# Convolution and low-rank mixer on one core: batch 0 cut in three pieces, index tables made between the loads, h of group 0 from four partial sums

## The chip, the core and the metric

The kernel runs on one core of a Trainium2 chip. The metric is device time in microseconds; the time before is the median of 11 runs, 331.04 us (330.2 to 332.82). One further execution was taken by the profiler and gave the trace; times "at 12.19" are microseconds from the start of its span. The core has TensorE (products, into eight PSUM banks of 128 x 512 fp32), VectorE, ScalarE and GpSimd (element work; GpSimd cannot be used on PSUM here and issues the loads that change type), and SyncE, which issues the other transfers. In the profile they are PE (PEld is its weight load), DVE, ACT, POOL and SP.

## The reference

`x` is 8 batches of 4224 rows of 192 numbers, in 8 heads of 24. A softmax over seven weights per head gives a causal convolution along the rows; its result `y` goes through a mixer of rank 32 over the rows and then a two-layer block per row:

```python
w = softmax(weight, axis=-1)                       # 8 heads x 7 taps
y[b, s] = sum over k of w[head, k] * x[b, s + k - 6]
h = y.transpose(0, 2, 1) @ U @ V                   # U 4224 x 32, V 32 x 4224
u = y + h.transpose(0, 2, 1)
out = u + maximum(u @ w_ch1, 0) @ w_ch2            # 192 -> 768 -> 192
```

The sum over rows in `y.T @ U` needs all of a batch's `y` before any `h` of that batch exists.

## The kernel before, in words

A batch is 33 tiles of 128 rows; eight tiles make a group, and 33 groups cover the eight batches. Group 0 and 1 hold tiles 0 to 15 of batch 0.

**Layout of x.** `x_sb` holds blocks of 64 rows: partitions 0 to 63 (r = 0) hold the first 32 blocks, partitions 64 to 127 (r = 1) the rest, plus one block of halo (L76 to L82). For batch 0 the loads are issued by GpSimd in pieces, `KP` (L86): tiles 0 to 12 of each half first, then the rest (tiles 13 to 15 of r = 0, 13 to 16 of r = 1).

**Queues.** The order of every engine is that of the program: nothing is rescheduled. GpSimd issues the two loads of the first piece (L95), makes the index tables with iota (L101 to L123), then issues U (L130, L134), the second piece of x (L135), V for groups 0 and 1 (L139), w_ch1 in four parts (L143), V for the rest (L153, L160), w_ch2 (L164) and batch 1 (L709). Its loads use eight completion semaphores in turn, so the ninth load waits until the first has landed, and so on. SyncE loads the weights (L61) and later only issues group transposes (L537) and outputs (L629).

**The convolution as products.** `hot` (L184) marks, from the tables `dif` and `tap`, where each tap stands in a 32 x 38 strip; `pr` is `hot` times the softmax weights, four heads at a time; seven products with the identity (L231) sum the taps in PSUM, and four ScalarE copies (L240) put the strips into `band`, a 128 x 128 matrix per head. `conv` (L368) multiplies `band` with blocks of x, 16 products of 64 x 64 per head for both halves of the partitions, and copies the result into `y_sb`: ScalarE for r = 0, VectorE for r = 1. Products of a zero tile (`idle`, L170) stand before the band and between band and convolution.

**U.** U is loaded with four rows in one partition; `u_layout` (L276) multiplies it with the selection matrix `Eq` (from the table `efp`) to get one row per partition, `U_sb`.

**Low-rank product.** `tt_mm` (L405) takes one product of 32 output rows per tile and puts them in turn in four column groups of the array, so that PSUM holds four partial sums in its four quarters of 32 partitions. For batches 1 to 7 `tt_split` (L421) writes them as a bf16 high part and low part, and `tt_sum` (L464) adds the quarters by products with `R4` (ones where two indices agree modulo 32) and copies the sum, repeated in all four quarters, to `tt_sb`. For batch 0 this is done otherwise: `tt_first` (L429) takes the first piece's 26 tiles, copies the partial sums to `tt_f` in fp32 and copies U of the last seven tiles four times side by side; after the rest of the convolution, an fp32 product with `R4f` (L701) and seven wide products (`tt_more`, L448) build the sum in PSUM, and `tt_done` copies it.

**Group 0 and 1.** `yT_part` (L542) puts the transposed `y` into three banks by products with the identity; `hT_part` (L558) adds h transposed there (V0_sb, 32 rows) and copies the sum to `uT`, one half by ScalarE, the other by VectorE. From group 2 on `h_group` makes u, and a DMA transposes it.

**The main loop** (L741): `w1` (L582) makes six pairs of 128 x 512 results per group, each reread with relu by ScalarE or VectorE; `w2` (L608) makes the output of two tiles, VectorE adds u, SyncE stores. An order written by hand (`SLOTS`) places the convolution and the low-rank steps of the next batches between these. After the first `w1` come `yT_part(1)`, `hT_part(1)` and h of group 2 (L753).

The start, which the edit rewrites, is this order:

Of the kernel before, what the change touches and what calls it, by code (L numbers as in the profile page):

```python
# [14 lines left out]
def kernel(  # L15
# [10 lines left out]
    nc = tc.nc  # L26
# [59 lines left out]
    KP = [(0, 13), (13, NB1 // 2)]  # L86

    def x_piece(k):
        for r in range(2):
            k0, k1 = KP[k]  # L90
            k1 = min(k1, (NB0, NB1)[r] // 2)
            x_part(0, r, (1 - r if k == 0 else 2 * k0 + 1), 2 * k1 + 1)

    x_tile(0)
    x_piece(0)  # L95
# [5 lines left out]
    dif = cst.tile([P, BW], F32, name="dif")  # L101
    for r in range(4):
        nc.gpsimd.iota(
            dif[QB * r : QB * r + QB, :],
            pattern=[[1, BW]],
            base=0,
            channel_multiplier=-1,
            allow_small_or_imprecise_dtypes=True,
        )
    tap = cst.tile([P, KC], F32, name="tap")  # L110
    nc.gpsimd.iota(
        tap[:],
        pattern=[[-1, KC]],
        base=HW,
        channel_multiplier=0,
        allow_small_or_imprecise_dtypes=True,
    )

    fp = cst.tile([P, P], I32, name="fp")
    nc.gpsimd.iota(fp[:], pattern=[[1, P]], base=P, channel_multiplier=-1)  # L120

    efp = cst.tile([P, 4, P], I32, name="efp")
    nc.gpsimd.iota(efp[:], pattern=[[-1, 4], [1, P]], base=4 * P, channel_multiplier=-4)  # L123
# [11 lines left out]
    x_piece(1)  # L135


    V0_sb = cst.tile([32, 2 * GT * P], BF16, name="V0_sb")
    nc.gpsimd.dma_start(out=V0_sb[:], in_=moe_V[:, 0 : 2 * GT * P])  # L139
    W1_sb = cst.tile([P, 3, M4], BF16, name="W1_sb")  # L140
    for m0, m1 in ((0, 2 * P), (2 * P, M4)):
        for hf in range(2):
            nc.gpsimd.dma_start(  # L143
                out=W1_sb[HB * hf : HB * hf + HB, :, m0:m1],
                in_=moe_w_ch1[:, m0:m1].rearrange("(c k) m -> k c m", k=HB),
            )

# [19 lines left out]
    zz = cst.tile([P, 512], BF16, name="zz")  # L167
    nc.vector.memzero(zz[:])  # L168

    def idle(n, w):  # L170
# [6 lines left out]
    idle(60, P)  # L177
# [5 lines left out]
    x_zero(0, nc.vector)  # L183
    hot = cst.tile([P, KC, BW], BF16, name="hot")  # L184
# [4 lines left out]
        op=ALU.is_equal,  # L189
    )  # L190
# [30 lines left out]
    def band_half(hh):  # L221
# [16 lines left out]
        for r in range(4):  # L238
            o = QB * (r % 2)
            nc.scalar.activation(  # L240
                out=band[QB * r : QB * r + QB, HQ * hh : HQ * hh + HQ, o : o + BW],
                in_=bp[QB * r : QB * r + QB, 0 : HQ * BW].rearrange("p (h t) -> p h t", h=HQ),
                func=ACT.Copy,
            )

    band_half(0)
    band_half(1)


    Eq = cst.tile([P, 4, P], BF16, name="Eq")  # L250
    nc.vector.tensor_scalar(
        out=efp[:], in0=efp[:], scalar1=P - 1, scalar2=None, op0=ALU.bitwise_and
    )
    nc.vector.tensor_scalar(
        out=Eq[:], in0=efp[:], scalar1=0.0, scalar2=None, op0=ALU.is_equal
    )
    nc.vector.tensor_scalar(
        out=fp[:], in0=fp[:], scalar1=R - 1, scalar2=None, op0=ALU.bitwise_and
    )
    R4f = cst.tile([P, P], F32, name="R4f")  # L260
    nc.vector.tensor_scalar(
        out=R4f[:], in0=fp[:], scalar1=0.0, scalar2=None, op0=ALU.is_equal
    )
    R4 = cst.tile([P, P], BF16, name="R4")
    nc.vector.tensor_copy(out=R4[:], in_=R4f[:])
# [10 lines left out]
    def u_layout():  # L276
        up = [bank() for _ in range(4)]
# [11 lines left out]
        for jj in range(4):  # L289
# [4 lines left out]
            )  # L294

# [72 lines left out]
    def conv(b, h0, nh, rs, engs, k0=0, k1=NT):  # L368
# [4 lines left out]
        pp = {r: bank() for r in rs}  # L373
# [31 lines left out]
    def tt_mm(b, js, p=None, o=0):  # L405
# [3 lines left out]
        for n, j in enumerate(js):  # L409
            c = n % 4  # L410
            nc.tensor.matmul(  # L411
                out=p[32 * c : 32 * c + 32, o : o + D],
                lhsT=U_sb[:, j // 4, j % 4, :],
                rhs=yt[b][:, j, :],
                start=(n < 4),
                stop=(n + 4 >= len(js)),
# [11 lines left out]

    def tt_first(p, js, rest):  # L429


        U4_sb = cst.tile([P, sum(b - a for a, b in rest), 4, R], BF16, name="U4_sb")
        n = 0
        for a, b in rest:
            nc.vector.tensor_copy(
                out=U4_sb[:, n : n + b - a, :, :],
                in_=U_sb[:]
                .rearrange("p k j r -> p (k j) r")[:, a:b, :]
                .unsqueeze(2)
                .to_broadcast([P, b - a, 4, R]),  # L440
            )
            n += b - a
        p = tt_mm(0, js, p, 256)
        t = sml.tile([P, D], F32, name="tt_f", bufs=1)
        evac("A", t[:], p[:, 256 : 256 + D])
        return U4_sb, t

    def tt_more(p, U4_sb, rest):  # L448
        js = [j for a, b in rest for j in range(a, b)]
        for n, j in enumerate(js):  # L450
            nc.tensor.matmul(
                out=p[:, 0:D],
                lhsT=U4_sb[:, n, :, :].rearrange("p a r -> p (a r)"),
                rhs=yt[0][:, j, :],
                start=False,
                stop=(n + 1 == len(js)),
            )
# [100 lines left out]
    def hT_part(g, tp, engs):  # L558

        uTt[g] = uts.tile([P, 4, 3, P], BF16, name="uT")  # L560
        for c in range(3):
            for hf in range(2):
                nc.tensor.matmul(
                    out=tp[c][HB * hf : HB * hf + HB, :],
# [234 lines left out]
```

## Time and profile before

| what | us |
|---|---|
| median of 11 runs | 331.04 (330.2 to 332.82) |
| the profiled execution | 329.99 |
| its span | 328.0 |
| first and second half of x land | 8.7 and 12.2 |
| band complete, first convolution product that has all of x's first piece | 11.14, 12.24 |
| first copy of uT of group 0 | 20.38 |
| first product of w1, group 0 | 21.27 |
| uT of group 1, first copy on the chain | 26.86 |
| first product of w2 | 32.30 |

The profile has a page (busy time per engine, the span in slices, DMA queues, the chain of work that ended last, the costliest groups of instructions) and views that answer questions: the chain in order of time (start, length, what), the instructions in order of time, groups by line and shape (count, busy time, mean ns of one), and for a line the durations of its instructions as least/median/greatest ns. A load's "to landing" counts from its issue.

### The profile page before, as it was taken

The page shows a single profiled execution, that of the slowest core. Times are in us where ns is not written, and L with a number is a line of the kernel's source. Part 1 is how long each engine was busy: PE and PEld are TensorE (multiplying, and loading weights), DVE is VectorE, ACT ScalarE, POOL GpSimd, SP SyncE. Part 2 cuts the span into 40 slices and gives each one's busy share as a digit, 9 for nine tenths or more (in the row PEclk, how much of TensorE's full clock was granted, in tenths as well). Part 3 has the DMA queues.
Part 4 walks back from the last instruction along what each step waited for, and adds up shares of the span by engine and source line. Part 5 has one row for each costly group of instructions (what it writes and reads, how often), then busy time and mean ns, then how long its engine had stood idle before and what let it go on. Part 6 is the DMA issues. An engine that isn't in the chain of part 4 may idle for free.

```text
span 328.0 us, 9736 instructions
## 1 busy us (share of the span) xinstructions
PE 318.6 (97%) x4072; PEld 224.5 (68%) x4072; DVE 268.5 (82%) x547; ACT 170.9 (52%) x351; POOL 142.1 (43%) x109
## 2 busy tenths in 40 slices
PE   7889999999999999999999999999999999999995
PEld 7655676567548746967874784587797497487494
DVE  5757999996986997898698799879897897896863
ACT  1658444662586098068529807833903902912910
POOL 8490229856993795967659598000000000000000
PEclk9999999999999999999999999999999999999999
DMA  8999996799999899699899969039569259259045
GB/s 99 192 164 166 165 208 153 144 193 164 244 176 231 144 204 190 175 218 182 170 222 155 203 172 199 27 98 250 65 128 218 91 144 215 78 129 258 3 131 160
DMA packets 122908, 53.54 MB, mean 163 GB/s; under 512 B 87760, under 2 KB 122832, under 8 KB 122864
## 3 DMA queue, kind: packets, MB, share of 16 engines
q1 hardware_dynamic: 84672, 38.18, 52.9%
q0 software_dynamic: 38192, 14.73, 39.5%
q8 instruction: 32, 0.52, 0.7%
q14 instruction: 12, 0.10, 0.1%
HBM read 29.49 MB, written 25.95 MB: 169 GB/s over the span
## 4 chain that ended last, share of the span: by engine, by line
PE 88%; DVE 4%; DMA 3%; ACT 3%; issue 1%; POOL 0%; DVEq 0%; POOLq 0%
PE ps L614 41%; PE ps L590 37%; PE ps L352 3%; DMA x_sb<-in_x_dram 3%; PE ps L496 3%; ACT rl_sb L601 2%; PE ps L411 2%; DVE y_sb L274 2%; DVE rl_sb L603 1%; DVE u_sb L518 1%; PE ps L381 0%; DVE out_sb L622 0%; POOL x_sb L79 0%; PE ps L467 0%; DVE uT L274 0%
## 5 line engine op out<-in xcount | busy, mean ns | idle before, releaser
L601 ACT ACTIVATE rl_sb<-ps 128x512 bf16<-128x512 f32 x235 | 125.3, 605 | 111.1 <-PE ps L590 99.1
L614 PE MATMUL ps<-W_sb,rl_sb 128*128 128x192 bf16 x1584 | 141.7, 246 | 0.1
L614 PEld LDWEIGHTS <-rl_sb 128*128 128x128 bf16 x1584 | 128.0, 98 | 13.4 <-issue 12.8
L590 PE MATMUL ps<-uT,W_sb 64*128 64x512 bf16 x1188 | 132.0, 376 | 0.8 <-DVE uT L274 0.8
L603 DVE TENSOR_SCALAR rl_sb<-ps 128x512 bf16<-128x512 f32 x161 | 104.3, 687 | 17.7 <-PE ps L590 17.4
L590 PEld LDWEIGHTS <-W_sb 64*128 64x128 bf16 x1188 | 64.2, 94 | 64.3 <-issue 5.0
L622 DVE TENSOR_TENSOR out_sb<-ps,u_sb 128x384 f32<-128x384 f32 (+1 forms) x133 | 70.1, 549 | 24.9 <-PE ps L614 24.5
L318 POOL COPY xb_sb<-x_sb 32x3072 bf16<-32x3072 bf16 (+1 forms) x24 | 67.6, 2824 | 0.7
L518 DVE TENSOR_TENSOR u_sb<-y_sb,ps 128x192 bf16<-128x192 bf16 (+1 forms) x168 | 66.2, 459 | 0.0
L306 POOL COPY xb_sb<-x_sb 128x3072 bf16<-128x3072 bf16 x12 | 32.8, 2742 | 30.6 <-DMA x_sb<-in_x_dram 12.9
L272 ACT ACTIVATE y_sb<-ps 128x384 bf16<-128x384 f32 (+3 forms) x90 | 36.8, 503 | 9.3 <-PE ps L352 6.8
L79 POOL DMA_DIRECT2D x_sb<-in_x_dram x32 | 27.1, 849 | 24.7 <-PE ps L590 14.4
L274 DVE CAST y_sb<-ps 128x408 bf16<-128x408 f32 (+2 forms) x42 | 20.8, 547 | 2.6 <-PE ps L381 2.6
L496 PE MATMUL ps<-tt_sb,V_sb 32*128 32x192 bf16 x264 | 12.6, 246 | 0.8 <-DVE tt_sb L461 0.6
L352 PE MATMUL ps<-x_sb,band 64*32 64x384 bf16 x192 | 12.1, 333 | 0.0
L352 PE MATMUL ps<-xb_sb,band 64*32 64x384 bf16 x192 | 12.1, 332 | 0.0
L496 PEld LDWEIGHTS <-V_sb 32*128 32x128 bf16 x264 | 4.7, 92 | 8.2 <-issue 8.2
L173 PE MATMUL ps<-zz 128*128 128x128 bf16 x90 | 7.8, 271 | 1.2 <-DVE zz L168 1.2
L173 PEld LDWEIGHTS <-zz 128*128 128x128 bf16 x90 | 7.6, 127 | 1.2 <-DVE zz L168 1.2
L425 ACT ACTIVATE tt_hi<-ps 128x192 bf16<-128x192 f32 x7 | 2.3, 330 | 10.8 <-PE ps L411 10.8
L381 PE MATMUL ps<-x_sb,band 64*64 64x312 bf16 (+3 forms) x192 | 7.2, 277 | 0.5 <-DMA x_sb<-in_x_dram 0.5
L352 PEld LDWEIGHTS <-band 64*32 64x32 bf16 x384 | 4.5, 89 | 4.1 <-issue 3.0
(64 smaller groups left out, 71.8 us busy)
## 6 DMA issues: line engine op xcount, KB each, us to landing
out_dram<-out_sb SPq DMA_DIRECT2D x131, 192.0 KB, 3.1
x_sb<-in_x_dram POOLq DMA_DIRECT2D x14, 384.0 KB, 7.8
x_sb<-in_x_dram POOLq DMA_DIRECT2D x7, 432.0 KB, 8.1
x_sb<-in_x_dram POOLq DMA_DIRECT2D x7, 408.0 KB, 9.0
x_sb<-in_x_dram POOLq DMA_DIRECT2D x1, 648.0 KB, 9.8
x_sb<-in_x_dram POOLq DMA_DIRECT2D x1, 624.0 KB, 7.4
uT<-u_sb SPq DMA_TRANSPOSE x31, 4.7
W_sb<-in_moe_w_ch_dram POOLq DMA_DIRECT2D x2, 192.0 KB, 5.9
```

Of the source, the lines that this page charges most:

```text
L272: nc.scalar.activation(out=out, in_=in_, func=ACT.Copy)
L274: nc.vector.tensor_copy(out=out, in_=in_)
L306: nc.gpsimd.tensor_copy(out=xbt[b][:, s0:s1, :], in_=xt[b][:, s0 + 1 : s1 + 1, :])
L318: nc.gpsimd.tensor_copy(out=xbt[b][q, s0:s1, :], in_=xt[b][q, s0:s1, :])
L352: nc.tensor.matmul(out=pp[r][QB * cg : QB * cg + QB, 0 : nk[r] * GS], lhsT=w[hr], rhs=t[hr, st : st + 2 * nk[r] - 1 : 2, hs], start=True, ...
L496: nc.tensor.matmul(out=banks[pr][:, a * D : (a + 1) * D], lhsT=V_sb[32 * q : 32 * q + 32, (j // 8) * 2 + j % 2, :], rhs=ttb[b][32 * q : 32 ...
L518: nc.vector.tensor_tensor(out=u_group(g)[:, i : i + n, :, hf, :], in0=yt[b][:, run[0] : run[0] + n, :].rearrange("p n (c k) -> p n c k", c=3),
L590: last = nc.tensor.matmul(out=pp[hf][:], lhsT=W1_sb[HB * hf : HB * hf + HB, c, m * P : (m + 1) * P], rhs=uTt[g][HB * hf : HB * hf + HB, :, ...
L601: nc.scalar.activation(out=rl[:, m, hf, :], in_=pp[hf][:], func=ACT.Relu)
L603: nc.vector.tensor_scalar_max(out=rl[:, m, hf, :], in0=pp[hf][:], scalar1=0.0)
L614: nc.tensor.matmul(out=cps[:, a * D : (a + 1) * D], lhsT=rlt[g][:, m, hf, (i + a) * P : (i + a + 1) * P], rhs=W2_sb[:, m, :], start=(m == ...
L622: nc.vector.tensor_tensor(out=o[:, 0:n, :].rearrange("p n (c k) -> p n c k", c=3), in0=cps[:, 0 : n * D].rearrange("p (n c k) -> p n c k", ...
```

## The change

- `KP` has three pieces: 8, 5 and 4 (r = 0: 3) tiles. `x_piece` now issues one half at a time.
- GpSimd issues the first half of piece one, makes `dif`, `tap` and `efp`, issues the second half, makes `fp`, and goes on with U and the pieces two and three. `dif` is one iota over all partitions; VectorE corrects it with `rq`, a small table of eight constants. `efp` is fp32 and is compared with `rq` in one step instead of a masking and a comparison.
- V for group 0 is loaded four times, once per quarter of 32 partitions; V for group 1 is loaded after w_ch1.
- The idle products are 100 of 16 columns and 34 of 128 before the band, 16 of 64 between its halves, and none after it (before: 60 of 128 and 30 of 128). The second half of the band is copied by ScalarE and VectorE in turn.
- Piece one is convolved two heads at a time; then come the transposes of group 0, `u_layout`, the low-rank product of piece one, the convolution of pieces two and three in the four banks that `u_layout` used, and their low-rank products into the same bank.
- Batch 0 uses `tt_split` too, and `hT_part(0)` multiplies the high and the low part, each with all four quarters (128 rows), by the four copies of V: the sum over the quarters happens in that product. `tt_sum(0)`, for h of all later groups of the batch, comes after the first `w1`. `tt_first` and `tt_more` are gone, and `R4` is made directly in bf16.

```diff
-    KP = [(0, 13), (13, NB1 // 2)]
+    KP = [(0, 8), (8, 13), (13, NB1 // 2)]
...
     x_tile(0)
-    x_piece(0)
+    x_piece(0, 0)
...
+    iota(dif[:], [[1, BW]], 0, -1)
     tap = cst.tile([P, KC], F32, name="tap")
+    iota(tap[:], [[-1, KC]], HW, 0)
+    efp = cst.tile([P, 4, P], F32, name="efp")
+    iota(efp[:], [[-1, 4], [1, P]], 0, -4)
+    x_piece(0, 1)
     fp = cst.tile([P, P], I32, name="fp")
     nc.gpsimd.iota(fp[:], pattern=[[1, P]], base=P, channel_multiplier=-1)
...
-    x_piece(1)
-    V0_sb = cst.tile([32, 2 * GT * P], BF16, name="V0_sb")
-    nc.gpsimd.dma_start(out=V0_sb[:], in_=moe_V[:, 0 : 2 * GT * P])
+    for k in (1, 2):
+        for r in range(2):
+            x_piece(k, r)
+    V0_sb = cst.tile([P, 2 * GT * P], BF16, name="V0_sb")
+    nc.gpsimd.dma_start(
+        out=V0_sb[:, 0 : GT * P],
+        in_=moe_V[:, 0 : GT * P].unsqueeze(0).to_broadcast([4, R, GT * P]),
+    )
...
+    nc.gpsimd.dma_start(out=V0_sb[0:R, GT * P :], in_=moe_V[:, GT * P : 2 * GT * P])
...
+    rq = cst.tile([P, 2], F32, name="rq")
+    for r in range(4):
+        for n, v in enumerate((32.0, -128.0)):
+            nc.vector.memset(rq[QB * r : QB * r + QB, n : n + 1], v * r)
...
-    idle(60, P)
+    idle(100, 16)
+    idle(34, P)
...
+    nc.vector.tensor_scalar(
+        out=dif[:], in0=dif[:], scalar1=rq[:, 0:1], scalar2=None, op0=ALU.add
+    )
...
+    Eq = cst.tile([P, 4, P], BF16, name="Eq")
+    nc.vector.tensor_scalar(
+        out=Eq[:], in0=efp[:], scalar1=rq[:, 1:2], scalar2=None, op0=ALU.is_equal
+    )
...
+    band_half(0, "A")
+    idle(16, 64)
+    band_half(1, "AD")
...
     def hT_part(g, tp, engs):
+        ts = ttb[0] if g == 0 else [ttb[0]]
+        k = P if g == 0 else R
+        for n, t in enumerate(ts):
+            for c in range(3):
+                for hf in range(2):
+                    nc.tensor.matmul(
+                        out=tp[c][HB * hf : HB * hf + HB, :],
+                        lhsT=t[0:k, HB * c : HB * c + HB],
+                        rhs=V0_sb[0:k, (2 * g + hf) * 4 * P : (2 * g + hf + 1) * 4 * P],
+                        start=False,
+                        stop=(n + 1 == len(ts)),
+                        tile_position=(0, HB * hf),
+                    )
...
-    idle(30, P)
-    for h in range(H):
-        conv(0, h, 1, [0, 1], "AD", *KP[0])
-    u_layout()
+    jb = NB0 // 2
+    js = [
+        list(range(k0, min(k1, jb))) + list(range(jb + k0, min(jb + k1, NT))) for k0, k1 in KP
+    ]
+    for h in range(0, H, 2):
+        conv(0, h, 2, [0, 1], "AD", *KP[0])
     yT = yT_part(0)
     ps0 = bank()
-    U4_sb, tf = tt_first(
-        ps0, list(range(KP[1][0])) + list(range(jb, jb + KP[1][0])), rest
-    )
-    for h in range(0, H, 4):
-        conv(0, h, 4, [0, 1], "AD", *KP[1])
-    nc.tensor.matmul(out=ps0[:, 0:D], lhsT=R4f[:], rhs=tf[:], start=True, stop=False)
-    tt_more(ps0, U4_sb, rest)
-    tt_done(0, ps0)
+    work = [bank() for _ in range(4)]
+    u_layout(work)
+    tt_mm(0, js[0], ps0, last=False)
+    for k in (1, 2):
+        for n, h in enumerate(range(0, H, 4)):
+            conv(0, h, 4, [0, 1], "AD", *KP[k], pp=work[2 * n : 2 * n + 2])
+    tt_mm(0, js[1], ps0, first=False, last=False)
+    tt_mm(0, js[2], ps0, first=False)
+    tt_split(0, ps0)
     hT_part(0, yT, "AD")
...
             if g == 0:
+                tt_sum(0)
                 hT_part(1, yT_part(1), "AD")
                 do("h2")
```

## The prediction

> **What bounds the kernel now.** I read the busy shares first, then the chain of work that ended last, then that chain for the first 30 us.
>
> ```profile
> span 328.0 us, 9736 instructions
> PE 318.6 (97%) x4072; PEld 224.5 (68%) x4072; DVE 268.5 (82%) x547; ACT 170.9 (52%) x351; POOL 142.1 (43%) x109
> ...
> PE 88%; DVE 4%; DMA 3%; ACT 3%; issue 1%; POOL 0%; DVEq 0%; POOLq 0%
> ```
>
> 88% of the chain is TensorE in the main loop, which the edit leaves alone. What it can move is the start; what the start wins or loses goes through to the end, as nothing later in the chain but TensorE and its evacuations ends a wait. The chain of the start:
>
> ```profile
> 2.38 9.81 DMA x_sb<-in_x_dram
> ...
> 12.24 0.47 PE ps L381 x6
> ...
> 12.72 2.44 DVE y_sb L274 x6
> ...
> 15.21 0.59 PE ps L281 x12
> 15.80 0.79 PE ps L548 x24
> 16.59 0.74 PE ps L411 x26
> 17.32 0.80 PE ps L381 x55
> ...
> 20.38 0.39 ACT uT L272
> ...
> 21.27 1.08 PE ps L590 x6
> 22.35 4.50 ACT rl_sb L601 x9
> 26.86 0.29 ACT uT L272
> ```
>
> Three things are to be seen. The second half of x (648 KB) lands at 12.19 and opens the convolution. VectorE's evacuations carry it to 15.2; U, transposes, low-rank product, rest of the convolution and h follow in series up to the first w1 product at 21.27, my mark. Then ScalarE carries the chain to 26.86, so a delay of group 1's uT there is a delay of all.
>
> **Loads.** Issue plus time to landing gives a curve of KB landed: 624 KB at 8.66 (1.26+7.4), 1272 at 12.2, with U 1536 at 13.8, with the last x 1872 at 16.2 (7.3+8.9), half of W1 (2192) at 17.7, all of it (2576) at 19.6. The first load is now 384 KB, whose issue takes 0.84 (row of 384 KB loads) against 1.12: the stream starts 0.3 earlier. The iotas now delay the second issue: one `dif` (at most 0.25, as `fp`), `tap` 0.15, `efp` 0.57 put it at 3.1 instead of 2.38; but 384 KB at the curve's 184 KB/us last 2.1 us from the first bytes near 3, so the stream doesn't run dry. Read off the curve less 0.3: the second half (792 KB) at 9.3, U (1056) at 10.7, the 5-tile piece (1536) at 13.5, the 4-tile piece (1872) at 15.9. V for group 0 comes in four copies (256 KB for 128, 64 more later): V0 at 17.1, W1 at 18 and 19.9. All are in time for steps at 18.3, 20.3 and 21.7 below. Each later Pool issue waits for the load eight before it; the latest such wait (W2 on W1's third part, about 19) gives W2 near 24, and its first use is at 32.3; batch 1's loads, issued from 19.0 and landed by 32.8, come about 1 us later, and are used from 40.7. SP's queue is not touched.
>
> By the Trainium skill ("DMA: Bandwidth & Descriptors", Anatomy of one DMA) each such load has a fixed 2.0 us, and the Bandwidth section advises 1 MiB or more: three added loads in series would be some 6 us, an estimate from that page. The trace disagrees for queued loads: the 144 and 192 KB pieces landed 0.7 us apart (15.5, 16.2).
>
> **Band.** `hot` starts at 4.60, after `tap`. Now `dif` is there at 2.4. VectorE first has eight tiny memsets (at most 0.14 each, the 64x96 row), band 0.48, x_zero 0.14, the add 0.22, `hot` 0.43, Eq 0.52: the reduction of w starts at 4.0 instead of 4.96. The chain behind it is unchanged, so `pr` starts at 5.75 and the band products near 7.1 and 8.25. Half the band is evacuated at 8.95 (four by 0.306); the other half, now on two engines, at 9.6 (before 11.14; VectorE's 32x152 copy is unseen, between the 0.2 of small copies and 0.41 of 128x256). So the load at 9.3 opens the convolution: 9.4 against 12.24.
>
> **First piece to the low-rank product.** 64 products of 192 columns lie between the rows of 72 (13.6 ns apart) and of 312 (43): 27, or 0.43 a call. Evacuations of 128x384 start at 10.0: ScalarE four by 0.42 (312 columns 0.34, scaled), to 11.7; VectorE four by 0.51 (1.02 for two), to 12.1. Transposes 11.75 to 12.4, U's products (0.75) to 13.15, U's evacuations 0.74 to 13.95, sixteen low-rank products at 31 ns to 14.45. TensorE stands still during U's evacuation, where the old order had the transposes.
>
> **Pieces two and three** share four banks, so the third waits for VectorE's copies of the second. Second: two calls of 0.45, to 15.35; copies of 128x480, 0.62 each by scaling 256 (0.37) and 384 (0.51), to 15.7 and 16.3. Third: 15.9 (load) and 16.35 (bank) to 16.8; copies to 17.05 and 17.6. Last low-rank products end at 17.95.
>
> **h from four partial sums.** Gone: the fp32 sum 0.59, the 7 wide products 0.81, tt_f and tt_sb. Added: hi 0.33 on ScalarE to 18.3, lo 0.34 on VectorE to 18.65, and six more products of 512 columns; the hi ones, three pairs by 0.213, run from 18.33 beside lo; the first lo pair (0.42 as L563's) ends at 19.4. 128 rows rather than 32 cost no more per product by the rows of L590 (64 rows, 512 columns, 376 ns) and L563 (32 rows, 382). First uT at 19.43 against 20.38: **-0.95**, so w1 starts at 20.3.
>
> **tt_sum(0) after w1(0).** Two products (0.17) ahead of group 1's transposes, and a copy (0.36) on VectorE behind w1's last relu, which ended 5.03 after the mark: tt_sb is there at +5.42, while L563 of group 1 began at +5.01 without waiting. Its uT can start 0.45 later (as 26.28 to 26.73), at +5.9; ScalarE was ready at +5.59 (26.86). Behind the waiting products stand h2 and w1(1). Cost between 0 (if the copy gets in ahead of the relu) and 0.44 (5.45 less 5.01): **+0.3**.
>
> At nothing: R4 without its fp32 step and the efp masking (VectorE idle from 10.7 to 12.7; if that cover goes, 0.6).
>
> **Sum** -0.95 + 0.3 = -0.65: profiled execution 329.99 (span 328.0 and 2.0 around) to 329.3. The median of the runs, 331.04, lies 1.05 above that execution; carried over: **330.4**.
>
> **The unseen cost: warm-up products.** 100 of 16 columns and 34 of 128 now stand before the band's products, due at 7.1.
>
> ```profile
> L173 PE MATMUL ps<-zz x12: 314/314/314, 2.8 to 4.0; 128*128 128x128 bf16 x12
> L173 PE MATMUL ps<-zz x47: 219/219/314, 5.8 to 11.3; 128*128 128x128 bf16 x47
> ```
>
> The granted clock column says full speed, but products take 314 ns up to 5.8 and 219 after; starts are 107 and about 58 apart. For a narrow product with a 128-column weight load the rows give 10.5 (64-column loads in four array quarters) to 107 ns, so 100 take 1 to 8 us (the last of them at the fast pace). I take 45, nearest to the 27 of L548, whose loads have 64 columns, doubled for the slow phase and less a little for the narrow product: the 100 end at 5.6, the 34 at 7.6. That is half a microsecond late, and hidden to the last tenth: the first half of the band is then evacuated at 9.45, the second, after 16 more idle products, at 10.2, and heads 4 to 7 begin at 10.26. The Trainium skill ("TensorE: Matmul & The Clock Gate", Part 1) gives half clock until some 3.4 us of activity, in free-running windows; the trace shows 4.6. It doesn't say whether 16 columns count as activity; an estimate by it, one more window at half clock, adds some 1.7 us to the 34.
>
> **Rivals.**
> 1. Slower: the warm-up. From an end at 7.6 on, the band and no longer the load opens the convolution, and each 0.1 us goes through. At 75 ns a pair 63 fit before 5.8, the other 37 (at 40) end at 7.3 and the 34 at 9.3: 1.7 late, total +1.05 (332.1); at 107 ns the end is 11.0, total +2.75 (333.8). For it: no row has a product so small behind a load so wide, and my 45 stands at the edge. Against: 32- and 64-column loads run at 21 to 27 ns in L411 and L548, and the load of 128 columns takes no longer in its row (98 ns) than that of 64 (106).
> 2. Faster: tt_sum costs nothing and the second half lands as early as 624 KB did (8.66 to 9.0). Then first piece 0.4 earlier, bounded by the last load at 15.9: -1.3 to -1.9 (329.1 to 329.7). For it: 792 KB is close to 624; against: VectorE's order puts the copy last.
> 3. The loads don't gain: the last x lands at 17.2, 1.0 after its old time, because the old 144 KB piece took 1.7 us behind U, and shorter pieces repeat that. Third piece at 17.2, w1 at 21.6 (4.4 behind, as from 15.9 to 20.3), total +0.6 (331.7): the edit doesn't do what it says.
>
> **Numbers.** Forecast 0.54 (own range 329.5 to 331.3; of it 0.24 below 330.05), rival 2 0.18, rival 1 0.19, rival 3 0.09. About 0.3% (1.0 us) is what a measurement of this kernel tells from no change. Faster 0.24+0.18 = 0.42; slower 0.19 and 0.01 of rival 3, 0.20; the rest 0.38. Range 329.0 to 332.4: rival 2's end to nearly all of rival 1 at 75 ns; 107 is left out.
>
> **What would show it.** The second x load landing near 9.3 and the first convolution product at 9.4; warm-up over by 7.6; uT's first copy at 19.4; the first w1 product at 20.3; a new wait of group 1's h on VectorE of about 0.4. Wrong if the convolution waits for the band, if the third piece waits for x beyond 16.3, or if the main loop (from 32 us on) changes its length.

## The result, and the profile after

The changed kernel took **333.58 us** (median of 12 runs, 332.52 to 334.33) against 330.98 us of the kernel before in the same session (47 runs): ratio 1.0067 [1.0049, 1.0086]. It is slower; forecast was 330.4, range 329.0 to 332.4. The profiled execution took 334.13, with a span of 332.4 us. Ratios, here and below, leave out executions more than 1.5% above the fastest of the same kernel: two of the ten of the kernel before with V0's load changed, and one of the twelve of that with split sums and an early sum.

The page's first lines, and the shares of the chain that ended last, answer to those shown of before:

```profile
span 332.4 us, 9999 instructions
PE 320.8 (97%) x4202; PEld 224.3 (68%) x4202; DVE 269.4 (81%) x553; ACT 170.9 (51%) x347; POOL 143.5 (43%) x109
...
PE 87%; DMA 4%; DVE 3%; POOL 2%; ACT 1%; issue 1%; POOLq 0%
PE ps L593 41%; PE ps L569 38%; DMA V_sb<-in_moe_V_dram 4%; PE ps L356 3%; PE ps L471 3%; PE ps L416 2%; POOL x_sb L79 1%; DVE rl_sb L582 1%; ACT rl_sb L580 1%; DVE y_sb L265 1%; DVE u_sb L493 1%; PE ps L442 0%; DVE out_sb L601 0%; POOL Ur L122 0%; PE ps L523 0%
```

Busy times are nearly those of before; TensorE is still 87% of the chain. But a load that did not stand there, V, now holds 4% of it. The chain in order of time (start, length, what) says which:

```profile
5.78 2.71 POOL x_sb L79 x4
8.49 11.97 DMA V_sb<-in_moe_V_dram
20.46 0.28 issue
20.74 0.53 POOL V_sb L151
21.27 2.04 DMA V_sb<-in_moe_V_dram
23.31 0.04 issue
23.34 5.54 PE ps L569 x36
```

The load of V0, the V of group 0, in four copies, issued at 8.49, takes 11.97 us to land, at 20.46; the forecast had 17.1. And w1 of group 0, my mark, starts at 23.34 rather than 20.3. (The second V load in the chain is one for later groups, which w1 does not read. It landed when VectorE's first copy of uT ended too, at 23.30, and the profile names whatever came last.) TensorE's instructions in order of time (start, busy, what; in brackets the idle time before it and what ended it), first h and w1 of group 0 of the kernel before, then the changed kernel:

```profile
19.93 0.83 PE L563 MATMUL ps<-V_sb,tt_sb 32*64 32x512 bf16 x6 [0.52 <-DVE tt_sb L461]
21.27 4.29 PE L590 MATMUL ps<-uT,W_sb 64*128 64x512 bf16 x36 [0.50 <-DVE uT L274]
```

```profile
16.13 0.22 PE L386 MATMUL ps<-x_sb,band 64*64 64x72 bf16 x2 [0.24 <-ACT y_sb L263]
17.34 1.17 PE L386 MATMUL ps<-x_sb,band 64*64 64x96 bf16 x62 [0.99 <-DMA x_sb<-in_x_dram]
18.45 1.13 PE L416 MATMUL ps<-y_sb,U_sb 128*32 128x192 bf16 x17
20.50 1.49 PE L541 MATMUL ps<-V_sb,tt_hi 128*64 128x512 bf16 x6 [0.93 <-DMA V_sb<-in_moe_V_dram]
21.73 1.54 PE L541 MATMUL ps<-V_sb,tt_lo 128*64 128x512 bf16 x6
23.34 5.54 PE L569 MATMUL ps<-uT,W_sb 64*128 64x512 bf16 x36
```

Three things are to be seen. The third piece stops after two of its 64 products, for 0.99 us. The products of h wait for V0. And they, like w1, are slow: the six of the high part take 1.49 (six took 0.83 before), and w1 5.54 (4.29 before). The windows of one microsecond (last three columns: granted clock, DMA share, GB/s) explain the last:

```profile
18.00:19.00 1.00, 0.88 (x60) 0.67 (x46) 0.77 (x2) 0.75 (x2) 0.13 (x1) 1.00 1.04 163
19.00:20.00 1.00, 0.52 (x7) 0.19 (x6) 0.27 (x2) 0.33 (x1) 0.00 (x0) 0.77 0.74 106
20.00:21.00 1.00, 0.50 (x4) 0.43 (x6) 0.34 (x1) 0.00 (x0) 0.26 (x1) 0.50 0.46 61
21.00:22.00 1.00, 1.00 (x8) 0.56 (x6) 0.00 (x0) 0.00 (x0) 1.00 (x3) 0.50 0.32 50
```

The clock is at 0.50 from 20 on (to 26), and the stream of loads, some 190 GB/s at a share of 1.6 while x came in, falls to 50 GB/s at 0.32, a quarter of the rate, although V0 (until 20.46) and, behind it, w_ch1 (W1, its last part until 23.2) are still wanted. The share adds up the times of all packets, so it can pass 1.

### The profile page after: what moved, and what is told of

Read it like the earlier page. It is cut to its first block, busy times and chain, and to the rows that moved or that the text cites. A ratio compares the mean times of both kernels' runs of the same rounds, so it can differ in the third digit from the quotient of the medians.

```text
span 332.4 us, 9999 instructions
## 1 busy us (share of the span) xinstructions
PE 320.8 (97%) x4202; PEld 224.3 (68%) x4202; DVE 269.4 (81%) x553; ACT 170.9 (51%) x347; POOL 143.5 (43%) x109
## 4 chain that ended last, share of the span: by engine, by line
PE 87%; DMA 4%; DVE 3%; POOL 2%; ACT 1%; issue 1%; POOLq 0%
PE ps L593 41%; PE ps L569 38%; DMA V_sb<-in_moe_V_dram 4%; PE ps L356 3%; PE ps L471 3%; PE ps L416 2%; POOL x_sb L79 1%; DVE rl_sb L582 1%; ACT rl_sb L580 1%; DVE y_sb L265 1%; DVE u_sb L493 1%; PE ps L442 0%; DVE out_sb L601 0%; POOL Ur L122 0%; PE ps L523 0%
## 5 line engine op out<-in xcount | busy, mean ns | idle before, releaser
L79 POOL DMA_DIRECT2D x_sb<-in_x_dram x34 | 28.2, 836 | 25.5 <-PE ps L569 16.1
L386 PE MATMUL ps<-x_sb,band 64*64 64x192 bf16 (+5 forms) x256 | 7.5, 249 | 2.4 <-DMA x_sb<-in_x_dram 2.1
L416 PE MATMUL ps<-y_sb,U_sb 128*32 128x192 bf16 x264 | 8.3, 248 | 0.7 <-DVE U_sb L265 0.5
L386 PEld LDWEIGHTS <-band 64*64 64x64 bf16 x256 | 5.6, 106 | 4.4 <-issue 2.9
L416 PEld LDWEIGHTS <-U_sb 128*32 128x32 bf16 x264 | 5.8, 96 | 2.6 <-issue 1.6
```

Source lines behind the costliest of these rows:

```text
L79: return nc.gpsimd.dma_start(out=xt[b][HB * r : HB * r + HB, s0:s1, :], in_=x[b, blk * HB : (blk + s1 - s0) * HB, :].rearrange("(j p) d -> ...
```

## The experiments

The theories at the start: **A**, V0's load with the copies as its outermost dimension uses only a few of the 16 DMA engines, lands late, and all behind it waits; **B**, x is late, because the stream runs dry between the two halves of the first piece; **C**, h from split sums costs more than it saves. Later ones are stated where they come up. Every median is of runs of its own beside the kernel before on the same chip.

**V0 in four loads** (the changed kernel otherwise).

```diff
-    nc.gpsimd.dma_start(
-        out=V0_sb[:, 0 : GT * P],
-        in_=moe_V[:, 0 : GT * P].unsqueeze(0).to_broadcast([4, R, GT * P]),
-    )
+    for q in range(4):
+        nc.gpsimd.dma_start(out=V0_sb[R * q : R * q + R, 0 : GT * P], in_=moe_V[:, 0 : GT * P])
```

> The changed kernel with V of group 0 loaded by four loads of 32 partitions each in place of one load with a leading broadcast of four. Theory A (the broadcast load is carried by few DMA engines, holds V0 and every load behind it, and TensorE falls to half clock while it waits): V0 lands before 18.5 instead of 20.5, the last part of w_ch1 before 21.5 instead of 23.2, no wait in front of h of group 0, the first w1 product near 22.0 instead of 23.3, w1 of group 0 back to 4.3 us from 5.5, total about 2.5 us under the changed kernel (331.1). Theory B (the late second half of x decides): only what stands behind V0 moves, under 1 us. Theory C (the split sums and the later tt_sum cost it): no change beyond 0.5 us.

331.22 us, ratio 1.0000 [0.9978, 1.0021]: within this interval all of the loss is gone, with the same bytes, in four loads of 32 partitions instead of one. They land from 17.7 to 18.3. TensorE in order of time:

```profile
16.15 0.22 PE L384 MATMUL ps<-x_sb,band 64*64 64x72 bf16 x2 [0.23 <-ACT y_sb L261]
17.52 1.03 PE L384 MATMUL ps<-x_sb,band 64*64 64x96 bf16 x62 [1.15 <-DMA x_sb<-in_x_dram]
...
20.03 0.84 PE L539 MATMUL ps<-V_sb,tt_hi 128*64 128x512 bf16 x6 [0.43 <-ACT tt_hi L428]
20.70 0.81 PE L539 MATMUL ps<-V_sb,tt_lo 128*64 128x512 bf16 x6
22.02 4.29 PE L567 MATMUL ps<-uT,W_sb 64*128 64x512 bf16 x36 [0.50 <-DVE uT L263]
```

The products of h wait for the high part, no longer for V0; the clock stays at 1.00, w1 is at 4.29 again. But the third piece's stop is still there, and the mark is 1.7 late against the forecast.

**V0 in one load of 32 rows**, tt_sum before h of group 0, and h from 32 rows.

```diff
-    nc.gpsimd.dma_start(
-        out=V0_sb[:, 0 : GT * P],
-        in_=moe_V[:, 0 : GT * P].unsqueeze(0).to_broadcast([4, R, GT * P]),
-    )
+    nc.gpsimd.dma_start(out=V0_sb[0:R, 0 : GT * P], in_=moe_V[:, 0 : GT * P])
...
-        ts = ttb[0] if g == 0 else [ttb[0]]
-        k = P if g == 0 else R
+        ts = [ttb[0]]
+        k = R
...
+    tt_sum(0)
     hT_part(0, yT, "AD")
...
-                tt_sum(0)
                 hT_part(1, yT_part(1), "AD")
```

> The changed kernel without the four partial sums in h of group 0: V0 is one load of 32 rows, tt_sum comes before h of group 0 and h is one product of 32 rows per half. Theory A: V0 lands by 17.5 and nothing waits for it; tt_sum's two products and copy (0.7) stand in the chain but six products fewer, so the first w1 product is near 22.3 and the later wait of group 1 is gone: about 331 in total, like the run with four loads. Theory C: this run gives back more than the run with four loads, by 0.5 us or more. Theory B: 1 us over before stays.

332.83, ratio 1.0048 [1.0024, 1.0071].

```profile
20.56 0.83 PE L538 MATMUL ps<-V_sb,tt_sb 32*64 32x512 bf16 x6 [0.45 <-DMA V_sb<-in_moe_V_dram]
21.90 5.62 PE L566 MATMUL ps<-uT,W_sb 64*128 64x512 bf16 x36 [0.50 <-DVE uT L262]
```

V0 landed at 16.3, so A's load is out of the way here; the V that the profile names is one of another group, and h began when tt_sum's copy was done (20.51). From the end of the third piece's stop (17.13 here, 17.52 with four loads) to w1 it took 4.77 us, against 4.50 with split sums. So C in its form "split sums cost" falls, by 0.3 us. The median is 1.6 us above that with four loads all the same, and the clock can account for most of it: it falls here too (0.50 from 22 to 25), so that w1 takes 1.3 us longer, 5.62, and all nine runs have a mean clock of 0.992 or less, where the ten with four loads have 0.995 or more. So V0 being late is not what it takes for the clock to fall.

**The kernel before with only V0's load changed** to the one with four copies.

```diff
-    V0_sb = cst.tile([32, 2 * GT * P], BF16, name="V0_sb")
-    nc.gpsimd.dma_start(out=V0_sb[:], in_=moe_V[:, 0 : 2 * GT * P])
+    V0_sb = cst.tile([P, 2 * GT * P], BF16, name="V0_sb")
+    nc.gpsimd.dma_start(
+        out=V0_sb[:, 0 : GT * P],
+        in_=moe_V[:, 0 : GT * P].unsqueeze(0).to_broadcast([4, R, GT * P]),
+    )
+    nc.gpsimd.dma_start(out=V0_sb[0:R, GT * P :], in_=moe_V[:, GT * P : 2 * GT * P])
...
-                    rhs=V0_sb[:, (2 * g + hf) * 4 * P : (2 * g + hf + 1) * 4 * P],
+                    rhs=V0_sb[0:R, (2 * g + hf) * 4 * P : (2 * g + hf + 1) * 4 * P],
```

> The kernel before with nothing changed but V0: loaded as four copies by one load with a leading broadcast of four, the second half loaded after w_ch1 as in the change; h still uses 32 rows. Theory A: V0 lands 11 to 12 us after its issue at 8.0 (about 20), w_ch1 at 20 to 23 instead of 17.1 to 19.6, the first w1 product is later by 0.5 or more and w1 of group 0 waits for weights or runs at half clock: 1 to 2.5 us slower than before (332 to 333.5). Theories B and C: no change (within 0.3 us).

334.62 (of all ten runs; 333.39 of the eight in the ratio), ratio 1.0083 [1.0043, 1.0122], with a wide spread even of the eight (332.12 to 336.55). h's products, which took 32 rows as before, wait for the load, and the stream falls to a quarter; TensorE, then two windows:

```profile
20.31 0.83 PE L567 MATMUL ps<-V_sb,tt_sb 32*64 32x512 bf16 x6 [0.62 <-DMA V_sb<-in_moe_V_dram]
21.64 5.98 PE L594 MATMUL ps<-uT,W_sb 64*128 64x512 bf16 x36 [0.50 <-DVE uT L278]
```

```profile
19.00:20.00 1.00, 0.69 (x7) 0.40 (x5) 0.35 (x2) 0.00 (x0) 0.00 (x0) 1.00 0.38 52
20.00:21.00 1.00, 0.69 (x6) 0.37 (x6) 0.15 (x1) 0.25 (x1) 0.45 (x1) 1.00 0.34 52
```

In this execution, the fastest of the ten, the wait itself costs little: the mark is 0.37 later (21.27 before), of which 0.27 stood there when the convolution began (12.51, before 12.24). The loss is w1 at half clock (0.50 from 23 to 26), 1.7 us longer. Still the one load makes either kernel slower, and taking it out makes the changed one even with the old: A stands, as to the late landing and as to the load being the cause; how much comes by waiting and how much by the clock is the next question. In both kernels the rate in and behind the wait is some 50 of 190 GB/s. The Trainium skill ("DMA: Bandwidth & Descriptors", Rules for kernel authors) has the rule for it: an outermost dimension smaller than 16, it names a leading broadcast of c copies, keeps the whole transfer on at most c engines. Four of 16 would be 48 GB/s of the trace's 190, an estimate; the trace agrees.

**What the half clock alone is worth**: V0's load kept, 16 idle products before h of group 0.

```diff
     tt_split(0, ps0)
+    for _ in range(16):
+        nc.tensor.matmul(
+            out=work[0][:, 0:P], lhsT=zz[:, 0:P], rhs=zz[:, 0:P], start=True, stop=True
+        )
     hT_part(0, yT, "AD")
```

> The changed kernel with V for group 0 still in one load with the leading broadcast, and 16 products of a zero tile (128 columns, 128 rows, extra work) between the copies of the split sums and the first product of h of group 0, so that TensorE does not stand still before V0 lands. In the changed kernel w1 of group 0 took 5.54 us at a granted clock of 0.50; in the kernel before 4.29 at 1.00. Theory A (V0's landing is the cause, at about 20.5): V0 lands at 20.5 as it did, h of group 0 starts with it, and the fill brings at most what the half clock cost: w1 of group 0 at 4.3 again, 332.4 to 333.0 against 333.6. Rival D (the half clock, from TensorE standing still, is most of the loss): w1 at 4.3 and no half clock from 19 to 26, 332.0 or less. If the clock falls all the same, it does not follow from the wait for V0, and the time stays at 333.6 or grows by the fill's own 1 us.

333.05, ratio 1.0043 [1.0021, 1.0065]. V0 landed at 21.04, the mark was 23.07, and w1 took 4.29 at full clock. So of the 2.4 us that four loads give back, about 0.8 is the clock (the difference of the two ratios, 0.0024; their intervals overlap, and V0 landed 0.6 later here, so it may be more), and the rest is the wait and what it shifts. The split differs from one execution to the next. In the profiled one of the changed kernel the wait moves h by 0.47 against four loads (20.50, 20.03), and the half clock then makes up 2.1 of the 2.57 us by which the first w2 product is later; but four of its twelve runs have a mean clock of 0.996 or more, and their median is 333.25. In the changed kernel the clock fell near 19.5 (0.77 in the window from 19), at the start of the wait for V0, not behind it; with four loads, and a stop of 1.15 at the third piece, it did not fall. What makes it fall is not settled.

**Both halves of x's first piece issued together**, in the changed kernel.

```diff
     x_piece(0, 0)
+    x_piece(0, 1)
...
     iota(efp[:], [[-1, 4], [1, P]], 0, -4)
-    x_piece(0, 1)
```

> The changed kernel with both halves of x's first piece issued ahead of the iotas. Theory B (the stream of x runs dry between the halves because the second is issued at 3.1): x's second half lands near 9.5 instead of 10.3, the dip in the transfer rate near 6.5 us is gone, and the last piece of x lands about 0.6 earlier; total 0.5 to 1 us less than the changed kernel. Theory A: the x loads move so, but h of group 0 still waits for V0 at about 20, so the total moves by less than 0.5.

332.34, ratio 1.0036 [1.0014, 1.0058]. B holds for the stream; window 6 to 7 of the changed kernel, then of this one:

```profile
6.00:7.00 1.00, 0.78 (x14) 0.66 (x12) 1.00 (x1) 0.00 (x0) 1.00 (x2) 1.00 1.09 103
```

```profile
6.00:7.00 1.00, 1.00 (x12) 1.00 (x11) 0.86 (x5) 0.00 (x0) 1.00 (x2) 1.00 1.61 202
```

The stream does run dry behind the first load, and here it doesn't: the last x lands at 15.7 instead of 17.3. But the iotas come later, so the band does (convolution at 11.0), and the mark is 22.79. V0, still in one load, landed at 19.9, before h asked for it at 20.8, and the clock stayed at 1.00. So the load costs h nothing here, and the median is 1.2 us below the changed kernel's, where the expectation from A was under 0.5. Still the third piece did not run through.

**Tables first**: four V0 loads, `dif` and `tap`, then both halves, then `fp` and `efp`, and VectorE's comparison for `Eq` after the second `pr`; and the same with **tt_sum before the first w1** (the last line of the diff, which the first version has not).

```diff
-    x_piece(0, 0)
...
     iota(tap[:], [[-1, KC]], HW, 0)
+    for r in range(2):
+        x_piece(0, r)
+    fp = cst.tile([P, P], I32, name="fp")
+    nc.gpsimd.iota(fp[:], pattern=[[1, P]], base=P, channel_multiplier=-1)
     efp = cst.tile([P, 4, P], F32, name="efp")
     iota(efp[:], [[-1, 4], [1, P]], 0, -4)
-    x_piece(0, 1)
-    fp = cst.tile([P, P], I32, name="fp")
-    nc.gpsimd.iota(fp[:], pattern=[[1, P]], base=P, channel_multiplier=-1)
...
     hT_part(0, yT, "AD")
+    tt_sum(0)
```

> The changed kernel with V0 in four loads of 32 partitions, and in GpSimd's order: dif and tap, then both halves of x's first piece one after the other, then fp and efp. It joins what the runs so far show: V0 loads that use all partitions land before h needs them, and with both halves together the stream has no gap at 6 us and the last x lands near 15.8 instead of 17.4. Theory (the rest of the loss is the last x piece, landing 1.5 late): last x at 15.8, third piece of the convolution at 16.1 to 16.3, w1 of group 0 at 20.6 to 20.9, total 330.1 to 330.6 against 330.9 of the kernel before. Rival F (once x is early, VectorE's chain to the band, or the copies between pieces two and three, set the time): third piece at 16.8 or later, w1 at 21.5 or later, total 331 or more.

> As the one before, and the sum over the quarters for the later groups (tt_sum) directly behind h of group 0 and before the first w1, so that its copy is not behind the relus. It adds two products of 192 columns (0.2 us) ahead of w1 and takes the wait of group 1's h on VectorE away. By the trace of the changed kernel uT of group 1 came 0.2 later after the mark than before; so the total is between 0.3 us less and 0.1 us more than the one before. If the copy of the sum on VectorE delays VectorE's half of uT of group 0, w1 starts 0.3 to 0.4 later and it is slower by as much.

331.22, ratio 0.9996 [0.9974, 1.0018], and 330.82, ratio 0.9978 [0.9959, 0.9998]. The second is the best version of the changed kernel, but not shown to be faster than the kernel before: its mark and first w2 product, at 21.50 and 32.53, are 0.2 later than there. Of the 35 runs of the kernel before beside it, 15 had a mean clock of 0.995 or less and took 331.37 or more, of its twelve two; the runs above 0.995 have medians of 330.85 and 330.77. And the theory behind the first was wrong. The last x landed at 15.6, as expected, and the third piece stopped all the same:

```profile
15.73 0.33 PE L385 MATMUL ps<-x_sb,band 64*64 64x72 bf16 x3 [0.24 <-ACT y_sb L262]
17.17 0.86 PE L385 MATMUL ps<-x_sb,band 64*64 64x96 bf16 x61 [1.11 <-issue]
```

"issue" is a wait for nothing that the profile shows: x, bank and copies were there. The kernel with 32 rows of V0 has the same stop behind the third product of that piece (0.74, to 17.13), that with the halves together too (0.41, to 18.45). In all of them one packet of a queue not shown so far, the instruction queue, began 2.2 to 2.5 us before the stop's end. The list of queues for 14.5 to 15.0 of the first version (packets, MB, share):

```profile
q8 instruction: 1, 0.02, 12.2%
```

12.2% of 16 engines for 0.5 us is 0.98 us of one DMA engine, for 16 KB. Hence **theory I**: TensorE ran out of instructions. In the program's order the products before the stop are 134 idle, 14 of the band, 16 idle, 64, 24, 16, 16, 64 and 3: it is behind product 351. Rival **J**: a wait for data that the profile misses.

**The place moved**: in the version with the early sum, 74 idle products fewer, or 30 more.

```diff
-    idle(100, 16)
-    idle(34, P)
+    idle(60, P)
```

```diff
+    idle(30, 16)
     for h in range(0, H, 2):
         conv(0, h, 2, [0, 1], "AD", *KP[0])
```

> The version with tables first, four V0 loads and the early sum, but 60 idle products of 128 columns before the band in place of 100 of 16 and 34 of 128: 74 products fewer on TensorE. In that version, and in the two others in which the last x landed by 15.9, TensorE stood still behind the third product of the third piece, product 351 in its order, until 17.1 to 18.5, waiting for nothing the profile names, while one 16 KB packet of the instruction queue ran from 14.7 to 15.9. Theory I (TensorE has run out of instructions: the next block comes late, and the place is fixed by the count of products): the stop moves 74 products later, behind some 13 of the 33 low-rank products of pieces two and three; the third piece runs through from 15.75 to 16.7; the instruction packet comes near 16.5 instead of 14.7, and the stop lasts to 2.3 us behind it, so the total gains nothing (330.8, between 330.2 and 331.5). Rival J (the stop is a wait for a bank, a copy or x of the third piece): it stays behind the third product of piece three and ends at 17.1.

> The version with tables first, four V0 loads and the early sum, with 30 more idle products of 16 columns (extra work) directly before the convolution, where TensorE waits 1.2 us for x anyway. Theory I: product 351 is now the 37th of the second piece's 64, so TensorE stops there (at about 15.1) with no wait that the profile names, and no longer behind the third product of piece three; time about as without (330.8), up to 1 us more if the next block is late too. Rival J: no stop in piece two, and the stop behind the third product of piece three stays.

With 30 more the stop is where the count puts it, to the product: behind the 37th of the second piece (30 products earlier in the work, 351 in the count), 2.3 us after an instruction packet at 13.8.

```profile
14.63 0.71 PE L385 MATMUL ps<-x_sb,band 64*64 64x120 bf16 x37
16.15 0.90 PE L385 MATMUL ps<-x_sb,band 64*64 64x120 bf16 x59 [0.81 <-issue]
```

With 74 fewer the third piece runs through, and the packet comes at 15.5:

```profile
15.46 1.22 PE L384 MATMUL ps<-x_sb,band 64*64 64x72 bf16 x64 [0.20 <-ACT y_sb L261]
16.61 0.81 PE L414 MATMUL ps<-y_sb,U_sb 128*32 128x192 bf16 x13
17.76 0.27 PE L414 MATMUL ps<-y_sb,U_sb 128*32 128x192 bf16 x4 [0.34 <-DVE y_sb L263]
...
20.45 4.29 PE L567 MATMUL ps<-uT,W_sb 64*128 64x512 bf16 x36 [0.23 <-DVE uT L263]
```

The short stop is behind 13 low-rank products (of 17; the 33 of the expectation counts piece one's too), but the 14th needs VectorE's copy, so here the place proves nothing. J falls by the other run, where a wait for data would have to hold the 38th product of the second piece, and the third piece no longer stops behind its third. The times: 330.91, ratio 1.0000 [0.9980, 1.0020] with 30 more; 331.44, ratio 1.0019 [0.9996, 1.0042] with 74 fewer, whose profiled execution is the fastest of its ten (329.59, mark 20.45); the other nine go up to 332.99, and four of the ten have a mean clock of 0.995 or less. The shorter warm-up seems to keep the clock less well; the next run tries it with nothing else but V0 in four loads.

**The shorter warm-up with only V0 in four loads**, to see whether the packet also delays x.

```diff
-    idle(100, 16)
-    idle(34, P)
+    idle(60, P)
```

> The changed kernel with V0 in four loads, and 60 idle products of 128 columns before the band in place of 100 of 16 and 34 of 128. With V0 in four loads alone, the last x landed at 17.5 and the third piece went on at 17.52, with the instruction packet at 15.3. If the packet, which holds one DMA engine for a microsecond, delays the last x load's share on that engine, the last x lands near 15.9 here, as the packet now comes later; the third piece then runs through from 16.2, and the stop is in the low-rank products behind it. If the last x lands at 17.3 or later all the same, its lateness is not from the packet, and the third piece waits as it did. Total 330.5 to 331.5 either way.

333.96, ratio 1.0098 [1.0074, 1.0121], of four runs, far above the 330.5 to 331.5 expected. The signs that it was made for came: last x at 16.2 instead of 17.5, third piece run through, and a stop behind product 351 (13 low-rank products on):

```profile
19.21 0.81 PE L413 MATMUL ps<-y_sb,U_sb 128*32 128x192 bf16 x13
20.83 0.27 PE L413 MATMUL ps<-y_sb,U_sb 128*32 128x192 bf16 x4 [0.82 <-issue]
```

VectorE's copy was done at 19.89, so this one is no wait for it, and the place is the count's again. That x was late because of the packet does not follow: with 32 rows of V0 a packet began at 14.9, and the last x landed at 15.9 all the same. What was not expected: the second half landed at 11.0 (10.2 with the long warm-up), TensorE stood still 1.0 and 1.8 us before that, the convolution ran at a clock of 0.50 from 12 to 14, and from 22 to 25 the clock was at 0.50 again. All four runs have a mean clock of 0.993 or less. Why that half was later, with no instruction packet in its way, stays open.

**The split sums on the old schedule**: the kernel before, V0 in four loads, h of group 0 from the four partial sums; tt_sum behind the first w1, then before it.

```diff
...
-    nc.tensor.matmul(out=ps0[:, 0:D], lhsT=R4f[:], rhs=tf[:], start=True, stop=False)
-    tt_more(ps0, U4_sb, rest)
-    tt_done(0, ps0)
+    tt_mm(0, js[1], ps0, first=False)
+    tt_split(0, ps0)
     hT_part(0, yT, "AD")
...
```

> The kernel before (two pieces, its order of loads and iotas), with h of group 0 from the four partial sums as in the change: tt_split, twelve products of 128 rows with four copies of V (loaded four times, 32 partitions each), tt_sum behind the first w1. It prices this one part of the change without its pieces. In the prediction the split sums take off the fp32 sum and the wide products (1.4 us of TensorE) and cost two copies and six products, so uT of group 0 comes at the old time or up to 0.4 us later here, where nothing else is late (the low-rank products of the last seven tiles now come before the split), and tt_sum costs 0.2 to 0.3 at group 1. Theory A plus this price: 331.0 to 331.7, ratio 1.000 to 1.002. Rival C (the split sums are themselves slower by 1 us or more): 332 or more, w1 of group 0 later than 22. Rival E (they gain): below 330.5, uT before 20.2.

> The kernel before with h of group 0 from the four partial sums (four V0 loads), and the sum over the quarters directly behind h of group 0 instead of behind the first w1. That version with the late sum took 330.95 against 331.37 of the kernel before. The early sum took 0.3 to 0.4 off in the other pair; so 330.6 here, ratio 0.996 to 0.998. If the two products and the copy delay uT of group 0, it is 331.2 or more.

330.95, ratio 0.9979 [0.9959, 0.9998], and 331.01, ratio 1.0018 [0.9993, 1.0042]. In the trace the split sums lose a little: mark at 21.60 and first w2 product at 32.95, against 21.27 and 32.30. The gain of the first version comes from elsewhere: it stands beside the same 35 runs of the kernel before, 15 of them with a mean clock of 0.995 or less; none of its ten had that. With V0 in four loads, this kernel does not have the loss that the load with four copies brought it. The early sum brings the w2 product to 32.69, but that doesn't show in the times, whose runs go from 330.05 to 333.61, with a twelfth at 335.01.

## Why the prediction was wrong

The step that failed is in **Loads**: "V0 at 17.1, W1 at 18 and 19.9. All are in time". It read every load off one curve of KB landed, as if each used the whole stream. V0 landed at 20.46, in a load that ran at a quarter of the stream's rate. This is worth 2.4 us of the 3.2 between forecast and result (four loads: 331.22). Part of it is a half clock in h and w1, for which the sum had no term. No rival held it. Rival 3 had a late x, and its last x at 17.2 came (17.3; its sign, the third piece waiting for x beyond 16.3, came too), but none had a late V0.

The other 0.8 (331.22 against 330.4) hides more. With V0 in four loads the mark is at 22.02 instead of 20.3, and the profiled execution took 331.32, 2.0 over the sum's 329.3. But the forecast added 1.05 to go from the profiled execution to the median, as it was in the kernel before; here the median lies 0.1 below that execution. That this term was wrong by 1.15 the other way is luck. The late mark has two terms:

| step | forecast | changed | V0 in four loads | tables first, early sum | 74 fewer |
|---|---|---|---|---|---|
| second half opens the convolution | 9.4 | 10.36 | 10.21 | 9.99 | 8.91 |
| low-rank product of piece one begins | 13.95 | 14.04 | 14.06 | 13.67 | 13.18 |
| third piece runs (from the stop) | 15.9 | 17.34 | 17.52 | 17.16 | 15.46 |
| h of group 0 | 18.33 | 20.50 | 20.03 | 19.51 | 18.46 |
| mark, w1 of group 0 | 20.3 | 23.34 | 22.02 | 21.50 | 20.45 |
| first product of w2 | | 35.94 | 33.37 | 32.53 | 31.48 |

- "The stream doesn't run dry": it did, at 6 to 7 us (103 GB/s). The half landed 1.0 late. Steps between it and the low-rank product were 0.9 shorter than summed, so this cost only 0.1 by 14.04.
- "Third: 15.9 (load) and 16.35 (bank) to 16.8": no term for instructions. In the changed kernel the last x landed at 17.3 and the block came then as well, so either explains its stop; with x early, the stop of 1.1 us remains. That is the second term. Whether the packet also made x late is not settled: without one near 15.3 x landed 1.3 earlier, but with one at 14.9 it was early too.
- Right in what followed, not in its price: the warm-up, the unseen cost. A product of 16 columns took 27 ns, not 45; the 134 products ended at 6.78 (forecast 7.6), and rival 1 didn't come. The band was complete at 10.4 (forecast 9.6, or 10.2 behind a warm-up to 7.6) and stayed hidden, but only because the half landed late: with 74 products fewer, where it landed at 8.9, heads 4 to 7 waited 0.34 for the band.

```profile
1.00 5.78 PE L176 MATMUL ps<-zz 128*128 128x16 bf16 x134 [1.00 <-DVE zz L166]
```

- Right in size: tt_sum behind w1. uT of group 1 came 5.79 behind the mark with four loads, 5.59 before: 0.2, forecast 0.3. Put before w1, the mark stays and w2 comes 0.33 earlier.
- Nearly right where it can be seen by itself: the chain of the start. In the run with 74 products fewer, V0 split and the tables first, every step is within 0.8 of the forecast, and the mark, 20.45, within 0.2. Its execution took 329.59; the sum, "329.3", was for such an execution. Part of this is luck: the steps up to the third piece came 0.4 to 0.8 early, and from there to h it took 3.00 us, not 2.43; and this execution is the fastest of ten whose median is 331.44.
- Wrong in part: "what the start wins goes through to the end". From the first w2 product to the end of the span the profiled executions took 295.6 to 297.4 us; with the tables first w2 came 0.5 earlier than with V0 split alone (32.86 against 33.37), and the median stayed, with a new wait of 0.45 for the transposed u of group 2, which travels beside batch 1's loads.

The runs leave open what makes the clock fall, and why the second half of x lands anywhere from 8.9 to 11.0.

## What to carry to other kernels

Work out each load's time from the engines it can use, not from the rate of the stream: look at its outermost dimension, and split a broadcast by partitions. Where short products follow each other by the hundred under heavy loads, count them: the supply of instructions is one more transfer, and a wait that the profile puts down to nothing ("issue") at the same product count in several versions is its mark. And test one part of a change on the old kernel as well as its removal from the new one.

## What the runs showed of the hardware that was not expected

- Once the other loads were done, one load with four copies outermost, and w_ch1 behind it, moved some 50 GB/s where the stream makes 190: in the changed kernel, and in the kernel before with this load (52).
- The instruction queue that follows TensorE's work brought packets of 16 KB, 33 for 4202 products, each holding a DMA engine for about 1 us; TensorE went on 2.2 to 2.5 us after a packet's start. The Trainium skill ("Runtime: NRT & Kernel Launch", Instruction fetch mechanics) has the 16 KB blocks, fetched while the current one is executed, and calls the cost mostly hidden. Here it was a stop of 0.4 to 1.1 us, seen in six versions, always behind product 351, where short products had run one behind the other while loads filled the DMA engines. That the stop is tied to the count is shown by moving it; that the packet is what ends it is argued from the times.
- Whether the same packets delay data is not settled. With tables first and the early sum, the second half of x landed 6.5 us after its issue with no packet before 11.8 (74 products fewer), and 7.6 with one at 6.2; but in the changed kernel's order, with V0 in four loads, it landed after 7.9 without a packet and 7.1 with one.
- The clock went to 0.50 for some 3 us where V0 was early, too (32 rows, 22 to 25), and stayed at 1.00 behind a stop of 1.15 us (four loads). What decides it is not known.
- A product of 16 columns behind a 128-column load took 27 ns in the first microseconds of the changed kernel, where one of 128 columns had started every 107 in the kernel before.
